# Another instruction order and another split of the copies in a recurrent forward chain

## Chip, cores, metric

One core of one Trainium2 chip runs the whole program. The metric is the device time of one execution in microseconds (us); lower is better. In the trace PE is the matmul engine and PEld its weight loads, DVE the vector engine, ACT the scalar engine, POOL the third elementwise engine, and SP the engine whose queue issues every DMA.

## The reference, cut to what matters

```python
for s in range(n_seg):                              # 64 steps, one after the other
    h = jnp.concatenate([mem, xs], axis=1)          # 8 memory rows + 32 input rows, 512 wide
    q, k, v = h @ Wq, h @ Wk, h @ Wv                # 32 heads of 128
    p = softmax(where(mask, q @ k.T * scale, -1e9))
    o = (p @ v) @ Wo
    mem = o[:, :8]                                  # the next step waits for this
    outs.append(o[:, 8:])
out = x + A(layernorm(x)) + B(layernorm(x))         # B is a dense layer
# returned: out, and the gradients of ten inputs
```

The memory rows make the forward pass a chain of 64 steps. The program runs the dense layer first, then this chain, then a block-wise pass without recurrence, then the backward chain, then the weight gradients.

## The kernel before

Inside the chain nothing is left to a scheduler. Every operation of a step has a short name, and strings say in what order they are written down; each engine runs its own operations in that order. Four strings, for the steps j=0 to 3 of a block, repeat 16 times. `L.` marks the "left" work: the memory rows of the block before, done once per block, not recurrent, and free to be put anywhere. A trailing `-` or `+` takes the operation from an earlier or later step (or block).

```python
F_ORDER = (
    "q0mm xt- L.lv L.ex0 ... soP- ... mx1 ex0 soV- sb1 soN ex1 v1mm ld- "            # j=0
    "v0mm su0 rc0 su1 rc1 pm0 L.ta- L.tb- ld tu0 pm1 tu1 kl+ v1ev L.lm v0ev L.ldL+ w0 L.xt- ob0 L.BT- oa0 "
    "L.rc1 soP L.tu0 w1 ob1 g0 oa1 g1 ra rb L.W0 L.out- L.oa0 L.ob0 ta tb HT",
    # ... j=1, j=2, j=3 cut
)
ENGS = on_engines(                                  # first list: ACT, second: DVE
    "L.oa0 L.oa1 L.ob0 L.ob1 k1Te k1ev oa1 ob0 q0ev q1ev ra v0ev v1ev",
    "L.pm0 L.pm1 L.ra0 k0Te k0ev oa0 ob1 pm0 pm1 q0Te q1Te rb")
```

The names that the argument uses, for halves 0 and 1 of the heads:

```python
# PE : q0mm..v1mm projections; q0fl.. transposes; s0 s1 scores; w0 w1 probabilities x values (f_pp);
#      g0 g1 output projection (ps_R); ta tb transposes of R (ps_sum)
# DVE: mx sb su rc pm = max, subtract, sum, reciprocal, product E; tu = 32x32 transposes, E -> ET
# ACT: ex = exp.    DVE or ACT by ENGS: *ev *Te copies; oa ob copies f_pp -> OT; ra rb copies ps_R -> R
# DVE: HT = reduction that writes the next step's memory rows X;  xt = the other rows, XT
# left work on PE: L.S0 L.S1 scores, L.W0 L.W1, L.G0 L.G1 (ps_RL), L.ta L.tb, L.BT (ps_rows)
# SP : ld loads f_vLs, which w0 needs; L.lm loads vM, which L.W0 needs; soV soN soP store N and E
def ld():                                           # of step s: loads for step s + 1
    if s + 1 < NSEG: load(s + 1)
E = fo.tile([P, KH, KW], BF16, name="E")            # one buffer for all steps
fpp: pool of one pair of PSUM banks                 # w1 waits until oa0 and ob0 have emptied w0's
```

## Time and profile before

Before: 3274.47 us, median of three runs (3266.94 to 3285.58). The profile is of another execution, which took 3253.77 us, less than any of the three. HT of the first 63 steps ends between 503.2 and 1352.1 us in the profile; this stretch, 849.0 us, is called the chain below. The windows view, for stretches inside the chain; the columns are busy time and instruction count of each engine, then the granted clock of PE (1.00 is full speed), DMA share and GB/s:

```profile
560.00:700.00 140.00, 122.75 (x2962) 66.18 (x2958) 87.56 (x259) 58.73 (x129) 8.86 (x22) 1.00 0.69 167
700.00:840.00 140.00, 123.17 (x2974) 66.22 (x2966) 90.15 (x271) 57.57 (x131) 8.05 (x20) 0.99 0.72 178
```

PE works 123 of 140 us. What a better order can win is the rest, so the places of the gaps matter. The timeline of PE in one step j=0 (start, duration, operation, count; in brackets the idle time before it and what ended it):

```profile
877.67 1.90 PE L434 MATMUL ps_proj<-Wqkv,X 128*32 128x512 bf16 x32
...
880.81 0.20 PE L562 MATMUL f_pp<-ET,f_N 32*128 32x32 bf16 x4 [0.65 <-DVE ET L468]
883.08 0.19 PE L562 MATMUL f_pp<-ET,f_vLs 8*128 8x32 bf16 x4 [2.07 <-DMA f_vLs<-S_NL]
...
884.31 3.51 PE L475 MATMUL ps_R<-Wo,OT 128*32 128x512 bf16 x32
...
888.35 0.90 PE L484 MATMUL ps_sum<-identF,R 128*128 128x128 f32 x4 [0.23 <-ACT R L418]
889.63 3.64 PE L434 MATMUL ps_proj<-Wqkv,X 128*32 128x512 bf16 x64 [0.38 <-DVE X L497]
```

w0 waits for the softmax chain (ET), then for a DMA (f_vLs). The last two gaps are the recurrence itself: R to `ta`, and HT to the next projections. In the j=2 step two steps earlier, w1 waits for the copy OT, in the same timeline view:

```profile
855.09 0.20 PE L562 MATMUL f_pp<-ET,f_N 32*128 32x32 bf16 x4 [0.57 <-DVE OT L421]
```

The 32 matmuls g0 and g1 on ps_R take 3.51 us here. In most steps they take 1.91. The windows view at this place says why; the last three numbers of a line are the clock, the DMA share and GB/s:

```profile
880.80:884.20 3.40, 1.32 (x68) 1.02 (x67) 2.07 (x9) 0.37 (x1) 0.00 (x0) 1.00 0.70 241
884.20:887.60 3.40, 3.40 (x59) 1.18 (x43) 0.58 (x2) 0.37 (x1) 0.00 (x0) 0.50 1.00 176
887.60:891.00 3.40, 2.76 (x68) 1.38 (x68) 1.85 (x5) 0.93 (x3) 0.00 (x0) 1.00 0.59 174
```

After 3.4 us in which PE was busy for 1.32, PE ran 3.4 us at half speed. The chain of this profile has four such half-speed windows, that is, records of a granted clock of 0.50.

### The profile page before, as it was taken

Reading aid. Unit: us, or ns where it says so; the run is one execution under the profiler, and the core shown is the slowest. Engines: PE = TensorE matmul, PEld = TensorE weight load, DVE = VectorE, ACT = ScalarE, POOL = GpSimd, SP = SyncE. Lnnn points to the kernel's source line nnn. Section 1 sums busy time; section 2 is a strip of 40 time slices with the busy share of each in tenths; the row PEclk is TensorE's granted clock in tenths of the full one; section 3 lists DMA queues with packets and bytes.
Section 4 is the critical chain, followed back from the end, with each engine's and each line's share of the span. In section 5 each row is a group of like instructions: output and inputs, shape, how many; then the busy total and the mean of one; then the engine's idle time right before and its main releaser. Section 6 shows DMA issues by size and latency. Waiting matters only on the chain. (4 is left out here: it accounts for less than half of the span.)

```text
span 3252.0 us, 113992 instructions
## 1 busy us (share of the span) xinstructions
PE 2723.4 (84%) x50873; PEld 1356.1 (42%) x50968; DVE 1332.7 (41%) x3765; ACT 952.7 (29%) x2316; POOL 193.7 (6%) x345
## 2 busy tenths in 40 slices
PE   8998778888888888834688888888888856999998
PEld 4453334444444444422344444443444423444443
DVE  4540035666666666623444554454455400010001
ACT  3331124444344444322333333333333301111111
POOL 0000000000000000000000010100000000000000
PEclk9999899999999999966799999999999978999999
DMA  9968894776767676799677767667766699999993
GB/s 255 282 146 314 292 294 116 169 181 173 174 172 184 170 186 167 205 227 251 164 181 187 173 179 204 165 167 181 192 173 169 183 246 190 207 195 219 181 182 94
DMA packets 890910, 633.11 MB, mean 195 GB/s; under 512 B 659745, under 2 KB 748466, under 8 KB 881074
## 3 DMA queue, kind: packets, MB, share of 16 engines
q1 hardware_dynamic: 890418, 625.81, 77.0%
q8 instruction: 400, 6.55, 0.9%
q14 instruction: 92, 0.75, 0.1%
HBM read 227.16 MB, written 250.10 MB: 147 GB/s over the span
## 5 line engine op out<-in xcount | busy, mean ns | idle before, releaser
L1363 PE MATMUL ps_gw<-gn,HNc 128*128 128x512 bf16 x1881 | 418.0, 381 | 8.1 <-ACT wt L1338 6.0
L434 PE MATMUL ps_proj<-Wqkv,X 128*32 128x512 bf16 x6144 | 356.6, 381 | 24.9 <-DVE X L497 24.1
L1363 PEld LDWEIGHTS <-HNc 128*128 128x128 bf16 x1920 | 188.7, 98 | 232.7 <-issue 11.0
L418 ACT CAST f_N<-ps_proj 128x512 bf16<-128x512 f32 x320 | 184.3, 584 | 241.3 <-PE ps_proj L434 222.5
L1338 ACT CAST wt<-ps_gw 128x512 bf16<-128x512 f32 x126 | 69.4, 591 | 550.7 <-DMA out_dram<-wt 333.5
L434 PEld LDWEIGHTS <-X 128*32 128x32 bf16 x6144 | 154.2, 97 | 180.7 <-DVE X L497 39.1
L1321 DVE TENSOR_TENSOR gx<-ps_rows,gb 128x512 f32<-128x512 f32 x16 | 11.1, 692 | 449.4 <-PE ps_rows L1319 418.7
L1363 PE MATMUL ps_gw<-GOc,gn 128*128 128x512 bf16 x627 | 141.0, 384 | 21.5 <-DMA gn<-S_ON 20.6
L475 PE MATMUL ps_gR<-WT,b_gv 128*32 128x512 bf16 x2048 | 144.8, 399 | 13.0 <-issue 12.9
L475 PE MATMUL ps_gR<-WT,b_gq 128*32 128x512 bf16 x2048 | 147.3, 400 | 8.3 <-issue 7.8
L475 PE MATMUL ps_gR<-WT,b_gk 128*32 128x512 bf16 x2048 | 149.7, 413 | 2.9 <-issue 2.8
L434 PE MATMUL ps_proj<-WoT,GT 128*32 128x512 bf16 x2048 | 123.6, 383 | 28.9 <-DVE GT L497 24.2
L484 PE MATMUL ps_sum<-identF,R 128*128 128x128 f32 x576 | 116.2, 297 | 24.6 <-ACT R L418 21.7
L418 ACT CAST gON<-ps_proj 128x512 bf16<-128x512 f32 x128 | 75.0, 586 | 185.2 <-PE ps_proj L434 185.2
L475 PE MATMUL ps_R<-Wo,OT 128*32 128x512 bf16 x2048 | 128.1, 393 | 0.0
L1142 POOL COPY b_vT<-b_vl 128x1024 bf16<-128x1024 bf16 x64 | 67.0, 1046 | 901.0 <-DMA b_vl<-S_A 459.1
L1363 PEld LDWEIGHTS <-gn 128*128 128x128 bf16 x640 | 63.3, 99 | 97.9 <-DMA gn<-S_ON 20.9
L403 PE MATMUL ps_L<-Wqkv,XL 128*128 128x512 bf16 x376 | 84.5, 384 | 18.5 <-DMA XL<-S_XL 16.9
L484 PEld LDWEIGHTS ps_sum<-identF,R 128*128 128x128 f32 x576 | 58.4, 141 | 97.0 <-ACT R L418 53.7
L421 DVE CAST b_gq<-b_pp 128x256 bf16<-128x256 f32 x128 | 54.4, 425 | 108.6 <-PE b_pp L562 105.0
L418 ACT CAST b_gk<-b_pp 128x256 bf16<-128x256 f32 x128 | 47.8, 373 | 173.8 <-PE b_pp L562 135.5
L418 ACT CAST b_gq<-b_pp 128x256 bf16<-128x256 f32 x128 | 47.7, 373 | 162.8 <-PE b_pp L562 153.0
(208 smaller groups left out, 4444.0 us busy)
## 6 DMA issues: line engine op xcount, KB each, us to landing
S_A<-f_N SPq DMA_DIRECT2D x64, 512.0 KB
out_dram<-wt SPq DMA_DIRECT2D x154, 128.0 KB
S_A<-f_N SPq DMA_DIRECT2D x64, 256.0 KB
S_ON<-OC SPq DMA_DIRECT2D x64, 256.0 KB
b_qN<-S_A SPq DMA_DIRECT2D x64, 256.0 KB
b_kN<-S_A SPq DMA_DIRECT2D x64, 256.0 KB
S_GB<-b_gv SPq DMA_DIRECT2D x16, 1024.0 KB
S_GB<-b_gk SPq DMA_DIRECT2D x16, 1024.0 KB
```

Of the source, the lines that this page charges most:

```text
L403: nc.tensor.matmul(ps[:], lhsT=XL[:, dc, q * P:(q + 1) * P], rhs=Wqkv[:, dc, c0:c0 + 512], start=(dc == 0), stop=(dc == DC - 1))
L418: nc.scalar.copy(out, in_)
L421: nc.vector.tensor_copy(out, in_)
L434: nc.tensor.matmul(ps[32 * g:32 * g + 32, :], lhsT=hT[:, dc, :], rhs=W[:, dc, c:c + 4 * P], start=(dc == 0), stop=(dc == DC - 1), tile_pos ...
L475: nc.tensor.matmul(R[32 * g:32 * g + 32, :], lhsT=XT(k, g), rhs=W[:, g * KH + k, :], start=(first and k == 4 * h), stop=(last and k == 4 * ...
L484: nc.tensor.transpose(st["T"][:, c * P:(c + 1) * P], R4()[:, c * P:(c + 1) * P], identF[:])
L1142: nc.gpsimd.tensor_copy(vT[:, :, :, 0:SEG], C["vl"][:])
L1321: nc.vector.tensor_tensor(out=gx[:], in0=ps[:], in1=gb[:], op=ALU.add)
L1338: nc.any.tensor_copy(wt[:], ps[:])
L1363: nc.tensor.matmul(ps[:], lhsT=l(rc), rhs=r(rc), start=(n == 0), stop=(n == RC_ALL - 1))
```

## The change

The intent: a search over a latency model wrote a new F_ORDER and ENGS for the forward chain. No operation is added or removed. The diff, cut to its core (j=2 and j=3 of the old strings and parts of the new ones are cut):

```diff
-            if c == 0:
+            if "T" not in st:
                 st["T"] = alloc("ps_sum")
...
     F_ORDER = (
-        ... mx1 ex0 soV- sb1 soN ex1 v1mm ld- "
-        "v0mm su0 rc0 su1 rc1 pm0 L.ta- L.tb- ld tu0 pm1 tu1 kl+ v1ev L.lm v0ev L.ldL+ w0 L.xt- ob0 L.BT- oa0 "
-        "L.rc1 soP L.tu0 w1 ob1 g0 oa1 g1 ra rb L.W0 L.out- L.oa0 L.ob0 ta tb HT",
...
+        "L.su0 q1ev q0ev k0ev k1mm soN- L.hs soP- k0fl L.rc0 k1ev soV- k0Te q0fl q0Te q1fl q1Te k1fl s0 k1Te mx0 "
+        "L.u2- sb0 s1 mx1 L.lm L.ldL+ sb1 ex0 su0 ld- soN-- v0mm rc0 L.mtr v1mm pm0 tu0 v0ev ex1 su1 w0 rc1 pm1 "
+        "km v1ev ob0 oa0 tu1 L.BT- L.su1 w1 ob1 oa1 L.pm0 L.rc1 g0 g1 L.pm1 ra L.tu0 rb ta tb HT",
+        "L.W0 q0mm q1mm ... k1Te s0 L.W1 soP- km mx0 sb0 s1 mx1 ex0 su0 sb1 L.lv+ rc0 L.oa1 "
+        "v0mm L.ob1 pm0 v0ev ex1 tu0 v1mm su1 v1ev w0 rc1 oa0 ob0 L.G0 L.u3 pm1 L.ra0 tu1 w1 g0 L.sx- soN oa1 ob1 "
+        "g1 ra ta rb tb HT",
+        "k1mm soN-- k0mm ... pm0 ex1 ld++ v1mm tu0 L.t0 su1 w0 v1ev L.G1 rc1 "
+        "pm1 tu1 oa0 ob0 w1 oa1 g0 ob1 L.lb g1 ra soV- kl+ ta rb tb HT",
+        ... rc0 pm0 v0mm v1mm tu0 su1 v0ev rc1 L.tb L.mst w0 L.ta "
+        "pm1 v1ev tu1 L.S0+ L.mx0+ ob0 oa0 w1 oa1 g0 ob1 L.xt g1 rb L.sb0+ ra L.S1+ L.mx1+ ta tb HT kl+ L.ex0+ "
+        "k0mm+ L.sb1+ xt q1mm+ L.t2 L.ex1+ q0mm+")
     ENGS = on_engines(
-        "L.oa0 L.oa1 L.ob0 L.ob1 k1Te k1ev oa1 ob0 q0ev q1ev ra v0ev v1ev",
-        "L.pm0 L.pm1 L.ra0 k0Te k0ev oa0 ob1 pm0 pm1 q0Te q1Te rb")
+        "L.oa0 L.oa1 L.ob0 L.ob1 L.ra0 k1Te k1ev oa0 ob0 ob1 q0ev q1ev ra v0ev v1ev",
+        "L.pm0 L.pm1 k0Te k0ev oa1 pm0 pm1 q0Te q1Te rb")
```

## The prediction

> **What bounds it now.** The change touches only the forward chain of 64 recurrent steps. In the trace, the reductions that write the next step's memory rows (L497, X; "HT") run from 503.2 to 1352.1 us: 849 us for 63 steps. In the windows view PE is busy for 122 to 124 us of every 140 us there at a clock of 0.99 to 1.00, DVE 87 to 90, ACT 57 to 58. So the stage is PE work plus short PE gaps at dependent places. A block of four steps took 54.9 us (mean of blocks 3 to 14); PE stood idle 6.4 us of it, so about 48.5 us is work that the change keeps. Gaps per block (timeline, waits): HT to the next projections 4 x 0.38; g1 -> ra -> ta about 0.53 in two or three steps; second outer product behind the copy OT 0.57 in two steps; the first behind the softmax chain (ET) 0.56 and 0.3; scores behind kT 0.2 in two; DMA (f_vLs, vM) and XT 0.9, in step j=0. Step times j=0..3: 14.2 (up to 17.3 when f_vLs is late), 13.1, 13.3, 13.2 to 13.9.
>
> **What the change does.** No instruction is added or removed. Moved:
> 1. Softmax: su1/rc1 come after pm0/tu0 on DVE, so ET0 is ready about 0.45 us earlier (su1 0.31, rc1 0.17 leave its chain); w0 can start 7.8 us after HT instead of 8.2.
> 2. The block's spare PE work fills gaps: G0 (1.05), G1, BT (0.66), S0 between w0 and w1, W0 (0.37) into an HT gap, W1 between s0 and s1, S1 before ta as before.
> 3. Both first-half OT copies go to ACT (0.37 each, in series, instead of one beside DVE's 0.43): hidden behind that filler.
> 4. j=0 loses W0 and the block rows' ta/tb and should fall to 13.1 us; W0, W1 and G0 crowd j=1.
> 5. f_vLs for j=0 is issued about 4.8 us before its use, not 3, but right behind a DMA transpose (1.4 us of issue).
> 6. j=3 evacuates rb before ra. The trace shows ACT and DVE taking the halves of R one after the other (DVE R waits on ACT R, 41 times); the Trainium skill, "PSUM — Partial Sum Buffer", Terms, says why: two engines must not use one bank at once. So ta waits for both, 0.5 us, partly covered by S1.
>
> **On the critical path.** Adding trace durations along each step (estimate): 13.1, 13.2, 13.05, 13.4, sum 52.8; from the other side, 48.5 of work plus 4.6 of gaps gives 53.1. That saves 1.8 us per block, about 28 us over 15.5 blocks, half of it the DMA wait in j=0. The Trainium skill, "Perfetto Trace Analysis", Optimization Strategy, says to find the gaps of the regime's busiest engine and what ends them. The trace agrees that PE is that engine (88%), so at most 6.4 us per block, 100 us in all, was to be had. The later stages just start earlier.
>
> **Predicted:** 3246 us, 8 in 10 within 3222 to 3270. Faster by over 2%: 0.05; within 2%: 0.92; slower by over 2%: 0.03.
>
> **What would show it.** Step times as in the sum; PE gaps per block near 4.6 us; no 0.57 gap before w1; w0 7.8 us after HT; few waits on f_vLs; later stages unchanged in length.
>
> **What would make it wrong.** The SP queue is in order: if soV's landing, which vM waits for, is late, then vM, the transpose and f_vLs follow, and j=0 stalls 2 to 4 us per block (+30 to +60 us). If w1 waits for ACT (v1ev, then two OT copies) or pm0 for the store of E, the gain of point 1 vanishes.

## The result, and the profile after

After: 3230.24 us, median of four runs (3226.02 to 3239.31), against 3274.28 before (now the median of four). A ratio in this document is the mean time of one kernel's runs over the mean of the other's of the same rounds, so it is not quite the ratio of the medians. Here it is 0.9866, 95% interval 0.9829 to 0.9903. Executions over 1.5% slower than the fastest of the same kernel are left out of the means. The predicted 3246 was 16 us too high; 3230 lies inside the range, and the gain of 1.3% is in the class that was given 0.92 (within 2%).

The windows view after, for the same two stretches:

```profile
560.00:700.00 140.00, 124.83 (x3024) 65.38 (x3028) 85.50 (x249) 61.89 (x144) 8.01 (x20) 1.00 0.77 185
700.00:840.00 140.00, 125.12 (x3116) 66.74 (x3110) 90.48 (x269) 64.69 (x150) 8.81 (x22) 1.00 0.72 175
```

PE is busy for two more microseconds of each 140. The timeline of PE at the end of the step j=0 that ends at 883.7 us, and the start of j=1:

```profile
878.41 0.20 PE L562 MATMUL f_pp<-ET,f_N 32*128 32x32 bf16 x4 [0.37 <-DVE ET L468]
...
879.75 0.20 PE L562 MATMUL f_pp<-ET,f_N 32*128 32x32 bf16 x4 [0.38 <-ACT OT L418]
...
880.06 1.91 PE L475 MATMUL ps_R<-Wo,OT 128*32 128x512 bf16 x32
882.50 0.90 PE L484 MATMUL ps_sum<-identF,R 128*128 128x128 f32 x4 [0.53 <-ACT R L418]
883.33 0.19 PE L562 MATMUL f_pp<-ETL,vM 32*128 32x32 bf16 x4
...
883.78 3.64 PE L434 MATMUL ps_proj<-Wqkv,X 128*32 128x512 bf16 x64
...
889.39 1.90 PE L434 MATMUL ps_proj<-Wqkv,X 128*32 128x512 bf16 x32
891.71 0.20 PE L562 MATMUL f_pp<-ET,f_N 32*128 32x32 bf16 x4 [0.42 <-DVE ET L468]
...
892.01 1.05 PE L475 MATMUL ps_RL<-Wo,OTL 128*32 128x512 bf16 x16
892.99 0.20 PE L562 MATMUL f_pp<-ET,f_N 32*128 32x32 bf16 x4
```

The DMA wait is gone, ps_R takes 1.91 again, and the projections at 883.78 follow without a gap (L.W0, at 883.33, fills it). Between w0 and w1 of j=1 stands L.G0 (ps_RL) with no gap after it (w1 starts at 892.99). The 0.53 before `ta` remains.

The chain in steps, worked out from the ends of HT; medians of blocks 3 to 14 in the first profile of each kernel, the mean of a block, and the gaps of PE over 0.05 us:

| | j=0 | j=1 | j=2 | j=3 | block, mean | PE idle per block |
|---|---|---|---|---|---|---|
| before | 14.30 (up to 17.32) | 13.12 | 13.30 | 13.55 | 54.90 | 6.42 |
| predicted | 13.1 | 13.2 | 13.05 | 13.4 | 52.8 to 53.1 | 4.6 |
| after | 13.21 | 13.24 | 13.14 | 13.54 | 53.28 | 5.67 |

Stage lengths in us, means of three profiles of each kernel (the first ones and two repeats in the experiments):

| stage | before | after | difference |
|---|---|---|---|
| start to the first HT | 506.2 | 509.5 | +3.3 |
| chain | 849.0, 849.9, 854.0: 851.0 | 825.1, 823.8, 824.6: 824.5 | -26.5 |
| last HT to the first backward projection | 232.4, 233.1, 233.9: 233.1 | 229.6, 227.8, 223.3: 226.9 | -6.2 |
| from there to the end | 1667.3 | 1663.5 | -3.8 |
| whole profile | 3257.6 | 3224.4 | -33.2 |

Of the four stages only the second and third differ in every pair; the first and last scatter by up to 13 us within one kernel.

### The profile page after: what moved, and what is told of

Same layout as the page of the kernel before. It is cut to its first block, busy times and chain, and to the rows that moved or that the text cites. A ratio compares the mean times of both kernels' runs of the same rounds, so it can differ in the third digit from the quotient of the medians.

```text
span 3237.5 us, 114125 instructions
## 1 busy us (share of the span) xinstructions
PE 2727.5 (84%) x50968; PEld 1349.2 (42%) x50968; DVE 1312.3 (41%) x3685; ACT 975.0 (30%) x2396; POOL 193.1 (6%) x345
## 4 chain that ended last, share of the span: by engine, by line
PE 60%; DMA 11%; SPq 11%; DVE 10%; issue 4%; ACT 3%; ACTq 0%; POOLq 0%; POOL 0%; DVEq 0%
PE ps_gR L475 12%; PE ps_proj L434 11%; PE ps_gw L1364 9%; SPq L1289 5%; PE ps_R L475 4%; PE b_pp L562 3%; PE ps_sum L484 3%; PE ps_tr L164 2%; DMA S_GOL<-l_gON 2%; PE ps_RL L1070 2%; DMA b_qN<-S_A 2%; DMA out_dram<-wt 2%; PE ps_w L363 2%; PE ps_w L383 1%; PE f_pp L562 1%
## 5 line engine op out<-in xcount | busy, mean ns | idle before, releaser
L1364 PEld LDWEIGHTS <-HNc 128*128 128x128 bf16 x1920 | 188.4, 98 | 237.4 <-issue 15.5
L475 PE MATMUL ps_gR<-WT,b_gv 128*32 128x512 bf16 x2048 | 148.3, 407 | 13.2 <-issue 12.9
L418 ACT CAST b_gq<-b_pp 128x256 bf16<-128x256 f32 x128 | 47.6, 372 | 163.4 <-PE b_pp L562 156.4
```

The lines of the kernel that those rows point to most:

```text
L418: nc.scalar.copy(out, in_)
L475: nc.tensor.matmul(R[32 * g:32 * g + 32, :], lhsT=XT(k, g), rhs=W[:, g * KH + k, :], start=(first and k == 4 * h), stop=(last and k == 4 * ...
L1364: nc.tensor.matmul(ps[:], lhsT=l(rc), rhs=r(rc), start=(n == 0), stop=(n == RC_ALL - 1))
```

## The experiments

Theory A was that of the prediction: the gain is the chain, shared between the DMA wait on f_vLs and better filled PE gaps. After the result it had an addition, that half-speed clock windows follow long waits. Its rivals: B, the excess over 28 us comes from elsewhere; C, the DMA wait hides other waits and is worth little; D and E, about the copy engines. A2 and B2 are forms of A and B. The half-speed windows are counted as records of the clock between the first and the last HT; where a record lasts 6.8 or 10.2 us, the number of 3.4 us windows stands in brackets. The chain and the windows are those of one profiled execution; the ratio is over all of them.

| run | ratio to before (95% interval) | chain | half-speed windows |
|---|---|---|---|
| before (first, e5, e12) | e5 0.9991, e12 0.9993 | 849.0, 849.9, 854.0 | 4, 5 (6), 7 (9) |
| after (first, e1, e11) | 0.9866; 0.9874 (0.9844 to 0.9904); 0.9879 (0.9846 to 0.9913) | 825.1, 823.8, 824.6 | 0, 0, 0 |
| e2 old, f_vLs early | 1.001 (0.998 to 1.0039) | 849.1 | 6 |
| e3 new order, old engines | 1.0013 (0.9967 to 1.0059) | 874.0 | 8 |
| e4 old order, new engines | 1.0004 (0.9969 to 1.004) | 849.3 | 1 |
| e6 new, f_vLs late | 0.9968 (0.9931 to 1.0005) | 863.7 | 9 (11) |
| e7 new, old softmax order | 0.9958 (0.9921 to 0.9995) | 847.4 | 0 |
| e8 new, two moves | 0.9932 (0.9908 to 0.9956) | 836.7 | 2 |
| e9 e8 with an earlier store | 0.9892 (0.9859 to 0.9926) | 823.6 | 1 |
| e10 new, ra first in j=3 | 0.988 (0.9851 to 0.991) | 823.2 | 1 |

All outputs are right.

### e1: the changed kernel again

No edit.

> Theory A: the whole gain lies in the forward chain (849.0 -> 825.1 us in the two profiles, first to last HT), so the ratio of times is about 0.992 (-24 to -28 us) once enough rounds are taken, and the 44 us of the first measurement is partly run-to-run spread of other stages. Rival B: the gain of 44 us (ratio 0.9866) is real and repeats, so some 20 us come from a place outside the chain that one pair of profiles does not show; then ratio 0.985 to 0.988 again. Profile: chain 824 to 827 us, step medians 13.2, 13.2, 13.1, 13.4, no wait on f_vLs, no half-clock window between first and last HT.

3224.33 against 3264.64 us, ratio 0.9874; chain 823.8 us, no wait on f_vLs, no half-speed window. The time gain repeats at 40 us and the chain gain at 25. Theory A's 0.992 lies outside the interval (0.9844 to 0.9904). So rival B is right that more is gained than the chain alone shows.

### e2: the old kernel with the f_vLs load of j=0 one step earlier

```diff
-        "... soN ex1 v1mm ld- " "v0mm su0 ...       # j=0
+        "... soN ex1 v1mm " "v0mm su0 ...
-        "... soV- ex0 L.t0 mx1 ...                  # j=3
+        "... soV- ex0 ld L.t0 mx1 ...
```

> The old order and copy engines, with one DMA moved: the load of f_vLs for step j=0 is issued in the step before. Theory A: of the 1.6 us per block that the change saves, about 0.5 to 0.6 is the wait for f_vLs itself and about 0.5 more the half-speed clock windows (3.4 us each, about 1.6 us of time) that follow its long waits; so j=0 falls to 14.2, the block from 54.9 to about 53.9, the chain to about 834 us, time -14 to -17 us, and no half-clock window stays in the chain. Rival C: the wait hides other work and something else (vM, ET, XT) binds next: less than 5 us gained.

No gain: 1.001, chain 849.1. Theory A failed here. The wait on f_vLs was gone (no idle time of PE was ended by it), but the same place then waited for something else. PE in one j=0 step of e2, timeline view:

```profile
939.74 0.20 PE L562 MATMUL f_pp<-ET,f_N 32*128 32x32 bf16 x4 [0.55 <-DVE ET L468]
...
940.60 0.92 PE L503 MATMUL ps_rows<-identF,XT 128*128 128x128 f32 x4 [0.49 <-DVE XT L491]
...
941.85 3.45 PE L475 MATMUL ps_R<-Wo,OT 128*32 128x512 bf16 x32
945.83 0.90 PE L484 MATMUL ps_sum<-identF,R 128*128 128x128 f32 x4 [0.23 <-ACT R L418]
```

L.BT (ps_rows) between w0 and w1 waits for the reductions XT on DVE. In the old order that wait lay behind the f_vLs wait. And this step, with no DMA wait at all, still ran ps_R at half speed: 3.45 us. Two short gaps, 0.55 and 0.49, came just before; of the 14 steps of e2 with these two gaps, 4 had a half-speed window. The wait on the other DMA, vM, grew as well, from 2.3 us in 6 matmul waits to 4.3 in 9; the steps of 14.9 to 15.5 us without a half-speed window are three of those. Rival C was right for the old order.

### e3: the new order with the old copy engines

```diff
-        "... L.ob1 L.ra0 k1Te k1ev oa0 ob0 ob1 q0ev q1ev ra v0ev v1ev",
-        "L.pm0 L.pm1 k0Te k0ev oa1 pm0 pm1 q0Te q1Te rb")
+        "... L.ob1 k1Te k1ev oa1 ob0 q0ev q1ev ra v0ev v1ev",
+        "L.pm0 L.pm1 L.ra0 k0Te k0ev oa0 ob1 pm0 pm1 q0Te q1Te rb")
```

> The new order with the old copy engines. Theory A: the DMA waits stay away, but the copy oa0, now on DVE again, stands behind tu1 in the new order and w1 waits for it, about 0.3 us per step: steps about 13.4 to 13.6, block about 54.2, time about +12 to +20 us against the changed kernel, so -10 to -30 against the old one. Rival D: the copy engines hardly matter and order alone gives all: block 53.3, time as the changed kernel.

The order alone is worth nothing: 1.0013, and its chain (874.0) is 49 us longer than after. The sign was right, the size far too small. Steps were 13.4, 14.6, 13.4 and 14.2 instead of 13.2, 13.2, 13.1 and 13.5. The loss in j=1 is in DVE's queue. Timeline of DVE in a j=1 step of e3, and then of PE:

```profile
851.05 0.32 DVE L549 TENSOR_TENSOR E<-sm_t,sm_rs 128x160 bf16<-128x160 f32 x1
851.65 0.69 DVE L421 COPY R<-ps_RL 128x512 f32<-128x512 f32 x1 [0.28 <-PE ps_RL L475]
852.26 0.43 DVE L468 STREAM_TRANSPOSE ET<-E 128x256 bf16<-128x256 bf16 x1
```

```profile
852.84 0.20 PE L562 MATMUL f_pp<-ET,f_N 32*128 32x32 bf16 x4 [1.24 <-DVE ET L468]
```

L.ra0 (R from ps_RL), on DVE again, waits for L.G0 and stands ahead of tu1 (ET), which needed only E. PE then idles 1.24 us before w1. In the changed kernel L.ra0 is on ACT and tu1 does not see it. In j=3 PE waits 1.01 us for a copy OT on DVE before w1: there it is oa0, behind tu1 and L.mx0 in DVE's queue (theory A had named tu1). No run moved L.ra0 or oa0 alone. Order and engine lists are one decision, and this half of it gains nothing.

### e4: the old order with the new copy engines

The same edit the other way round, on the old kernel.

> The old order with the new copy engines. Theory A: both first-half OT copies on ACT in series and no filler between w0 and w1 in j=1 and j=2: w1 comes about 0.3 us later there, block +0.6 to +1.2 us, time +8 to +20 us against the old kernel; f_vLs waits as before. Rival D: no effect, within 4 us of the old kernel. Rival E: the copy engines carry the gain: -10 us or more.

The steps did what theory A said: 14.13, 13.38, 13.56, 13.41, so w1 came 0.26 us later in j=1 and j=2. Undisturbed steps add up to about 0.65 us more per block than before, but the chain did not grow (849.3), because this execution had 5 waits on f_vLs (3.6 us) instead of 7 to 9 (7.7 to 8.6) and one half-speed window instead of four to seven. The time did not move either (1.0004); whether for the same reason is not shown, as only one of the four executions was profiled. Over the whole program their granted clock was 0.935 to 0.939, that of before 0.931 to 0.938. The number of half-speed windows is a term of its own, and it is partly chance.

### e5 and e12: the kernel before again

> The kernel before, unchanged, for a second profile. [...] Theory A2: how many there are differs from run to run by where the grid falls, and the first profile (4 windows in the chain, 849 us, run time at the low end of its kind) had few; this one has 4 to 10 and a chain of 849 to 860 us. Rival B2: the chain repeats at 849 +- 2 us, and the other 15 us of the 41 measured come from the stages after it.

> The kernel before, third profile: chain 849 to 850 us, 4 to 6 half-speed windows in it, ratio 1.000 +- 0.003. If the stages after the chain take longer here by 8 us or more than in the changed kernel's profile on this chip, that is rival B's second stage; if they agree within 5 us, the difference is spread between executions.

("How many there are" means the half-speed windows. In the first profile of before one followed a window in which PE was busy for 0.70, and none followed others at 0.58 and 0.62.) Chains of 849.9 and 854.0 us with 5 and 7 half-speed windows. Both fit A2's ranges, and 854.0 lies outside B2's 849 +- 2 and outside e12's 849 to 850. But the chain of before repeats within 5 us, so a lucky first profile cannot explain the other 15 us, and B2 is right in that. From the last HT to the first backward projection it took 233.1 and 233.9 us.

### e6: the changed kernel with the f_vLs load of j=0 late

```diff
-        ... sb1 ex0 su0 ld- soN-- v0mm rc0 L.mtr v1mm pm0 ...
+        ... sb1 ex0 su0 soN-- v0mm rc0 L.mtr ld- v1mm pm0 ...
```

> The changed kernel with one DMA moved: f_vLs of step j=0 is issued after the transpose vTM, about 2 us before its use as in the old kernel, not 4.8. Theory A2: waits on f_vLs of 0.5 to 3 us come back in j=0, and because the gaps then pile up in one place half-speed windows come back too; chain +20 to +40 us, time +15 to +40 us against the changed kernel. Rival C: the wait is absorbed as it was in the old order (moving the load there gained nothing): under +5 us.

Chain 863.7 us, 39 us over after, and 9 half-speed windows. The profiled execution was the slowest of its four (3270.09; the others 3241.37 to 3258.13). What PE waited for on f_vLs, weight loads and matmuls both counted:

```profile
  DMA f_vLs<-S_NL: 45.7, 28
```

That is 22.2 us of matmul waits in 14 steps, about 1.6 us each. Nine windows at about 1.55 us (worked out in the section on the prediction) make 14 more, as an estimate. So theory A2 holds for the new order: here nothing as long stands behind the load. In this execution moving it back costs more than the chain's whole gain; by the ratios, 0.9968 against 0.987 to 0.988, it costs about 30 of the 40 us.

### e7: the changed kernel with the softmax order of before

In each of the four strings su1, rc1 and ex1 go ahead of pm0 and tu0 (in j=3 ex1 already stood there); j=2 as the example:

```diff
-        ... su0 rc0 v0ev pm0 ex1 ld++ v1mm tu0 L.t0 su1 w0 v1ev L.G1 rc1 " "pm1 tu1 ...
+        ... su0 rc0 ex1 su1 rc1 v0ev pm0 ld++ v1mm tu0 L.t0 w0 v1ev L.G1 " "pm1 tu1 ...
```

> The changed kernel with su1 and rc1 ahead of pm0 and tu0 on DVE again (and ex1 ahead of v0ev on ACT), as in the old order. Theory A: ET0 is ready 0.45 us later, w0 starts 8.2 to 8.3 us after HT instead of 7.83; w1 follows its filler, so steps grow by 0.1, 0.3, 0.4, 0.4: block +1.0 to +1.3, chain +16 to +20 us, and perhaps some half-speed windows. Rival C: w1 is bound by ET1, which is not later, so the block grows by under 0.4 us.

Chain 847.4, 23 us more than after (16 to 20 expected); steps 13.42, 14.00, 13.49, 13.63. PE's wait for ET alone grew from 0.42 to 1.19 us in j=1 and from 0.52 to 0.93 in j=2. A j=1 step of e7 in the timeline of PE:

```profile
897.49 0.20 PE L562 MATMUL f_pp<-ET,f_N 32*128 32x32 bf16 x4 [1.19 <-DVE ET L468]
```

There was no half-speed window although PE idled 7.3 us per block, more than in before. That fits gaps which are spread, but the profiled execution was the fastest of its four (3226.99; the others 3246.17 to 3252.90) and had the highest clock (0.942 against 0.933 to 0.939), so the others may have had some. Rival C falls.

### e8, e9, e10: further moves

e10 changes the end of j=3; e8 does the same and also moves L.W1; e9 is e8 with the store of E issued first in j=2.

```diff
-        ... g1 rb L.sb0+ ra L.S1+ L.mx1+ ta tb HT kl+ ...        # j=3: e8, e9, e10
+        ... g1 ra L.S1+ ta rb L.sb0+ tb HT L.mx1+ kl+ ...
-        ... s0 L.W1 soP- ... L.lv+ rc0 L.oa1 " "v0mm L.ob1 ...   # j=1: e8, e9
+        ... s0 soP- ... rc0 " "v0mm ...
-        "k1mm soN-- k0mm ... L.otr ... soP- s0 ...               # j=2: e8
+        "L.W1 k1mm L.oa1 L.ob1 soN-- L.lv+ k0mm ... L.otr ... soP- s0 ...
+        "L.W1 k1mm L.oa1 L.ob1 soP- soN-- L.lv+ k0mm ... L.otr ... s0 ...   # j=2: e9
```

> Two further moves on the changed kernel: j=3 evacuates ra before rb again, with L.S1 and ta between, and L.mx1 after HT; and L.W1 goes from between s0 and s1 of j=1 into the gap before the first projection of j=2. Theory A: j=3 loses 0.15 to 0.2 us (the gap before ta), j=1 loses 0.16 (w0 7.83 instead of 7.99), the others stay: block 52.9 to 52.75, chain -5 us, time -3 to -6 us, which 5 rounds may not resolve but the step times will. Rival: W1 in the gap delays the projections or its copies delay k1ev on ACT, and j=2 gains what j=1 loses.

j=3 fell from 13.36 to 13.15 in its undisturbed blocks, as expected. But j=2 rose to as much as 16.87 (with a half-speed window in it), and the kernel lost 12 us of chain. The tile view of E names the wait, the timelines of DVE and SP show one such place:

```profile
  DMA S_A<-E: 12.8, 8
```

```profile
581.56 0.33 DVE L549 TENSOR_TENSOR E<-sm_t,sm_rs 128x160 bf16<-128x160 f32 x1 [2.34 <-DMA S_A<-E]
```

```profile
573.57 1.50 SPq L571 DMA_TRANSPOSE qL<-S_NL  x1
575.19 2.64 SPq L755 DMA_TRANSPOSE ON<-OTL  x1
577.93 0.53 SPq L877 DMA_DIRECT2D S_A<-E  x1
```

E has one buffer. L.W1 later means L.oa1 and L.ob1 later, so the transpose ON, which reads their tile, stood longer in the in-order queue, and the store of E behind it was issued when pm0 already wanted to write E.

> The previous kernel with the store of E issued at the start of j=2, ahead of the two transposes that delayed it. There pm0 of j=2 waited for that store in 8 steps, 12.8 us in all, and each wait drew PE idle time and twice a half-speed window. Theory A: with the store early these waits go; j=0..3 take 13.21, 13.21, 13.14, 13.15, block 52.75 to 52.9, chain 818 to 822 us, no half-speed window. Rival: another store or load of the in-order queue now comes late and stalls a step.

With the store early the waits of j=2 went, and the chain is 823.6 us. It is not the 818 to 822 expected: j=1 gained 0.03 instead of 0.16, because a gap of 0.19 before s1 opened where L.W1 had been, and one half-speed window fell in.

> The changed kernel with the j=3 move alone (ra before rb, L.S1 and ta between, L.mx1 after HT). Theory A: j=3 13.36 -> 13.15 as in the kernel with both moves, everything else as in the changed kernel: block about 53.0, chain 820 to 822 us, time -3 to -5 us against the changed kernel on the same chip.

j=3 13.15 in undisturbed blocks, chain 823.2 (820 to 822 expected; one half-speed window fell in); the time equals that of the changed kernel on the same chip (3231.01 and 3231.26 us). A saving of 0.21 us in each of 16 blocks is below what the times resolve. None of the three beats the changed kernel clearly.

### e11: the changed kernel a third time

> The changed kernel once more, beside the kernel before in the same call, for the size of the gain and for stage lengths on one chip. Theory A: chain 824 +- 1.5 us and ratio 0.988 to 0.992. Rival B: ratio 0.985 to 0.988 again, and then the profile pair shows a second stage that differs by 8 to 15 us.

Chain 824.6. The ratio, 0.9879 (0.9846 to 0.9913), lies on the border of the two theories and does not tell them apart. The stage lengths do, with e12: rival B again. The second stage that differs is the one after the chain: 223.3 us against 233.9. SP issues the load of WoT, which the next stage needs, in the last block. Timeline of SP, before and then after:

```profile
1370.80 0.39 SPq L888 DMA_DIRECT2D WoT<-S_WOT  x1
1371.31 8.85 SPq L710 DMA_TRANSPOSE OC<-OT  x1
```

```profile
1351.49 0.38 SPq L889 DMA_DIRECT2D WoT<-S_WOT  x1
1351.91 0.43 SPq L876 DMA_DIRECT2D S_A<-f_N  x1
```

Counted from the last HT that is 18.7 us before and 15.1 after; 19.5 and 19.7 against 15.6 and 15.2 in the repeats. The stretch in question has a DMA share of 0.78 to 0.97 in before and 0.63 to 0.99 in e11, so the earlier load was taken for the cause of a stage 3 to 11 us shorter. The other traces speak against it as the whole cause. All nine profiles with the new order issue this load 15.1 to 15.7 us after the last HT, and their stage takes 223.3 to 233.3 us; in e3 the load was early (15.5) and the stage took 233.3, as long as the 232.4 to 233.9 of the five profiles with the old order. The first matmul on WoT also comes only 1.4 us earlier in the mean (51.0 to 52.4 us after the last HT against 52.3 to 54.2). What shortens this stage stays open: no run moved this load alone.

## Why the prediction was right or wrong

**The time.** It was right in direction and inside its range, but the gain was sized at 28 us and measured at 40 to 44 (by the three ratios; 37 to 44 by the medians). The missing terms are these.

- **The chain: 28 forecast, 26.5 measured.** This sum held: the steps came out within 0.15 us of 13.1, 13.2, 13.05 and 13.4. In part that was luck. The sum had no half-speed windows in it, because they were not known, and none fell in the chain of after; and the share of it that was put down to the DMA wait was wrong, as told below.
- **"The later stages just start earlier" failed.** The stage after the chain is 6.2 us shorter in the mean of three profiles, in every one of them. Together with the scattered rest the profiles differ by 33.2 us, the times by 40 to 44 over more executions; what the remaining 7 to 11 us is stays open. The times of one kernel on one chip scatter by up to 30 us, and the first profile of before was a quick execution (3253.77 us), so it need not be a further cause.

**"Half of it the DMA wait in j=0" failed.** Taking that wait out of the old kernel gained nothing (e2), since XT, vM and the clock stood behind it: a step j=0 of before took 14.20 us with a wait of 0.42 us on f_vLs and 14.20 with none but 0.49 on XT. A wait at one instruction is not a term of a sum while another wait ends just before it.

**What was overlooked: the clock.** The mean clock of 0.99 to 1.00 over 140 us was read as "full speed". It hid windows of 3.4 us at 0.5. Two steps j=0 of before with the same waits and no DMA wait show the price alone: 15.76 us with such a window, 14.21 without, so 1.55 us. Their ps_R in the timeline:

```profile
1102.93 3.43 PE L475 MATMUL ps_R<-Wo,OT 128*32 128x512 bf16 x32
...
1158.76 1.91 PE L475 MATMUL ps_R<-Wo,OT 128*32 128x512 bf16 x32
```

The Trainium skill, "TensorE: Matmul & The Clock Gate", "What's actually happening", says that a block watches PE in free-running windows of 3413 ns and switches between half and full clock. The trace agrees: nearly all records are multiples of 3.4 us, and in each profile the edges of the half-speed windows in the chain fold onto one grid of 3.413 us to within 1 ns.

With it the chain's 26.5 us can be divided, as an estimate from these numbers: undisturbed steps fell from 14.20 + 13.12 + 13.30 + 13.20 = 53.82 to 13.21 + 13.24 + 13.14 + 13.36 = 52.95 us per block, 14 us over the chain; 5.3 windows (counted as records) at 1.55 us are 8; the other 4 to 5 are DMA waits and small disturbances. All of the 14 comes from j=0 (-0.99 per block); j=1 to j=3 change by +0.12, -0.16 and +0.16. The old order piled its gaps up in j=0 (ET 0.55, XT 0.49, f_vLs). The new one spreads them, and no window fell in any of three executions.

**The PE gaps** were forecast at 4.6 us per block and measured at 5.67, while the "48.5 us" of work became 47.6. Half-speed matmuls had been counted as work that the change keeps: three windows in blocks 3 to 14 are about 0.4 us per block (estimate); the other 0.5 stays open.

The six points of the change:

1. Softmax order: right, and undoing it inside the new order costs 23 us of chain (e7). w0 comes 7.83 to 7.99 us after HT (forecast 7.8; before 8.44, 8.21, 8.40 and 8.24 in j=0 to 3). No run put it alone into the old order.
2. Fillers: right. The gap before w1 in j=1 and j=2 is gone, and one HT gap is filled. But the filler takes its own time: from w0 to w1 it is now 1.28 and 1.34 us there instead of 0.94, and in j=3 1.34 instead of 1.00, which takes back most of the earlier w0.
3. The OT copies in series on ACT: hidden, as forecast. The forecast did not name L.ra0, which goes to ACT as well: without the new engine lists the order is worth nothing (e3), and in j=1 the trace of e3 puts that on L.ra0.
4. j=0 at 13.1: 13.21.
5. f_vLs: right that the lead suffices. No PE gap of the first two profiles of the changed kernel is ended by it (0.2 us in the third), and taking the lead away costs 39 us of chain in the slow execution that was profiled, about 30 by the ratios (e6).
6. rb before ra in j=3, with L.S1 and L.mx1 where they stand, costs 0.21 us per block (e10 moves all of them). The prediction cited the Trainium skill, "PSUM — Partial Sum Buffer", Terms, for why the halves go one after the other. The trace agrees in that the second copy waits for the first (DVE R on ACT R, 68.8 us in 47 waits in the chain after); that the bank is the reason was not tested.

## What to carry to other kernels

Before a wait is priced, ask what waits stand behind it at the same place: removing the last of several frees nothing until the others move as well. An engine list and an order for in-order queues belong together, and a stall can come from an operation that only stands ahead in the same queue. A mean clock near 1.00 does not rule out half-speed windows (four here at 0.99 to 1.00), so look for them in short windows. That the same idle time costs fewer of them when it is spread fits e7 and the changed kernel, but no run moved gaps with the idle time held fixed.

## What the Trainium skill lacked or had wrong

- "TensorE: Matmul & The Clock Gate", "HAM oscillation": it states the abstract rule as no PE idle gap over about 3.4 us. Here a gap of 2.07 us (in the step of before that is shown) was enough, and in e2 gaps of 0.55 and 0.49 us in one step were in 4 of 14 cases. By a grid of 3.413 us laid over the traces, PE was busy for 0.17 to 0.74 of the window ahead of each switch. In the chain every window under 0.48 was followed by half speed, but one at 0.48 (e8) and many from 0.54 up were not. So busy share as the profile models it is no sharp threshold.
- "Perfetto Trace Analysis", "Optimizing Scalar/DVE Operations": it advises moving work from DVE to ACT by load and breaking up instructions that cause bubbles; this section does not say that the place in the queue decides. Moving copies alone gained nothing (e4), and with the new order a copy of 0.69 us on DVE held up a ready transpose and cost PE 1.24 us of idle (e3).
- "DMA: Bandwidth & Descriptors" gives no time for which one DMA transpose holds SP's queue on trn2 (only cycle counts of "previous generations", in a table for a later chip); here it was 1.2 to 3.6 us inside the chain of before and after and up to 8.85 us behind the large WoT load. In e8 a store of E behind two transposes came late and stalled DVE (2.34 us at the place shown).
